# Clustered attention in front of two expert blocks: the cluster chain computed in PSUM, and a new order of the attention

## The chip, the cores and the metric

The kernel runs on one core of a Trainium2 chip. TensorE (PE) multiplies matrices into PSUM; VectorE (DVE), ScalarE (ACT) and GpSimd (POOL) work element by element; SyncE's queue (SP) issues the transfers. The metric is the device time of one execution in microseconds (us), as the median of several.

## The reference

Three parts follow one another. The first is attention for 2 batches x 8 heads, 768 tokens of 64 numbers, in which a query sees only the keys of its own cluster:

```python
q_assign = argmax(q_n . c_n)      # 16 centroids per head
k_assign = argmax(k_n . c_n)
mask = q_assign[:, None] == k_assign[None, :]
scores = where(mask, scale * q @ k.T, -1e9)
attn = softmax(scores);  out = attn @ v
```

The second is a mixture of experts: each of the 1,536 tokens (512 numbers) goes to the best of 8 experts (512 to 1024, relu, back to 512), and is weighted by two gates. The third is a dense layer pair (512 to 2048 and back) with a piecewise quadratic activation. All products use pairs of fp16 numbers (a high and a low half), so that their sums come close to fp32.

## The kernel before

**The attention** has 16 heads (`NH`), of which each goes through these steps, with 768 tokens as 6 tiles (`NT`) of 128:

- `load_kq`, `load_v`: SP loads k, q and v. `kq_hi` (ACT) rounds k and q to fp16, `kq_lo` takes the rest (fp32 minus fp16, 768 numbers per partition). `v_hi` and `v_lo` do the same for v (384 numbers). `a_dma` transposes the halves, `dup` copies the high halves into the tile `kq`.
- `logits`: PE multiplies with the centroids into `LG`, 192 columns of the PSUM tile `m_bank` (12 groups of 16 clusters: 6 of k, 6 of q). The same bank also holds the router's logits `LGX`, its ranks `RK` and one column `ZC`.
- `assign`, **the cluster chain** on DVE: the largest logit (L391), where it is reached (L394), times falling weights (L397), the largest of these, which is the first index (L400). From this q gets a one-hot row (L404) times 32768 (L406), and k the difference to its largest (L405). The results go into 16 columns of `kq`, and `b_dma` transposes the tile to `bT`.
- `s1`, `s1_max`: PE computes the masked scores of a tile of queries and DVE takes their maximum (L421, `mq`). `aug`, three DVE instructions on six columns (L426, L429, L431), turns the maxima into two more columns of `kq`; `q2_dma` transposes them.
- `st`: PE computes the scores again, transposed and with the maximum subtracted; `p_exp` (ACT) takes the exponential; `p_hi` (ACT or DVE) and `p_lo` (POOL or DVE, L462) split it into fp16 halves; `pv` multiplies with V, and `evac` (DVE, L492 to L496) divides by the sum and stores to `x_all`.

After head 8 the first batch is routed (`xsplit`, `xt_dma`, `lgx`, `gating`, `scatter`), after head 16 the second. Then the buffers of the attention are closed, and the experts and the dense layers follow.

**The order** of the attention's instructions comes from a planner, the class `Steps`, which runs while the program is built. Each step has a rank, engines that could take it with a duration each (`alts`), the steps it waits for, and places in rings of buffers that it takes and frees (`RINGS`; `lg`, the place of the logits, is 1). The planner keeps a clock for each engine, takes among the steps that could start within `eps` of the earliest the one with the lowest rank, and moves a step to its second engine where this ends it earlier by more than `gain`. The ranks are head number times 6 plus a constant of the kind of step (`R`) and a correction of single heads (`OFF`). Each engine executes its instructions in the order in which the planner issued them, and waits with semaphores for the others.

Of the kernel before, what the change touches and what calls it, by code (L numbers as in the profile page):

```python
# [30 lines left out]


class Steps:

    def __init__(self, rings):
        self.ready, self.order = [], []
        self.cap, self.freed = rings, {r: [] for r in rings}

    def add(self, rank, alts, fn, deps=(), take=(), free=(), lat=0.12, cols=None):


        o = dict(cols=cols, rank=rank, alts=alts, fn=fn, wait=0, at=0.0, take=take, free=free, lat=lat, next=[], end=None, slot={})
        for d in deps:
            if d is not None:
                d["next"].append(o)
                o["wait"] += 1
        if not o["wait"]:
            self.ready.append(o)  # L50
        return o

    def run(self, eps, gain):
        self.gain = gain
        busy, count, tick = {}, {}, 10.24 / 3
        while self.ready:
            pick = {}
            for o in self.ready:
                at = o["at"]
                for r in o["take"]:  # L60
                    f, n = self.freed[r], len(self.freed[r]) - self.cap[r]
                    if n >= 0:
# [15 lines left out]
            d = o["alts"][e]  # L78
# [41 lines left out]
def build(tc, q, k, v, centroids, w_gate, w_og, w1, w2, w_in, w_out, out):  # L120
    nc = tc.nc
# [248 lines left out]

    def dup(i):
        nc.vector.tensor_copy(out=kq[i % NKQ][:, :, :, 0:D].rearrange("p z t d -> p t z d"), in_=a_t[i][:, :, 0::3, :])

# [14 lines left out]
    def assign(i):  # L388

        mx = sm.tile([128, 2 * NT, 1], F32, tag="mx", name="mx")  # L390
        nc.vector.tensor_reduce(out=mx, in_=LG, axis=AX.X, op=ALU.max)  # L391
        yield
        eq = sm.tile([128, 2 * NT, NCL], F16, tag="eq", name="eq")
        nc.vector.tensor_tensor(out=eq, in0=LG, in1=mx.to_broadcast([128, 2 * NT, NCL]), op=ALU.is_equal)  # L394
        yield
        w = sm.tile([128, 2 * NT, NCL], F16, tag="w", name="w")
        nc.vector.tensor_tensor(out=w, in0=eq, in1=wt.to_broadcast([128, 2 * NT, NCL]), op=ALU.mult)  # L397
        yield
        m2 = sm.tile([128, 2 * NT, 1], F16, tag="m2", name="m2")
        nc.vector.tensor_reduce(out=m2, in_=w, axis=AX.X, op=ALU.max)  # L400
        yield
        oh = sm.tile([128, NT, NCL], F16, tag="oh", name="oh")
        x = kq[i % NKQ]
        nc.vector.tensor_tensor(out=oh, in0=w[:, NT:], in1=m2[:, NT:].to_broadcast([128, NT, NCL]), op=ALU.is_equal)  # L404
        nc.vector.tensor_tensor(out=x[:, 0, :, D:KS1], in0=w[:, 0:NT], in1=m2[:, 0:NT].to_broadcast([128, NT, NCL]), op=ALU.subtract)  # L405
        nc.vector.tensor_scalar(out=x[:, 1, :, D:KS1], in0=oh, scalar1=32768.0, scalar2=None, op0=ALU.mult)  # L406
        yield
# [15 lines left out]
    def aug(i, ts):  # L423

        m1 = sm.tile([128, NT, 1], F32, tag="m1", name="m1")[:, ts]
        nc.vector.tensor_scalar(out=m1[:, :, 0], in0=mq[:, i, ts], scalar1=-(2.0 ** 22), scalar2=-LN8 / SCALE, op0=ALU.max, op1=ALU.add)  # L426
# [364 lines left out]
    T = Steps(RINGS)  # L791
    R = dict(ld=-58.49, spl=-21.9, as_=-13.26, s1=-12.92, st=0, pv=3.78, hi=39.69, lo=30.55, v=31.52, la=4, rt0=23.34, rt1=-59.11, rt2=-5.38, l0=3)

    def chain(rank, gen, times, deps, fused, free):

        if fused:
            return T.add(rank, {"DVE": sum(times) + 0.13 * len(times)}, lambda e: [0 for _ in gen], deps, free=sum(free.values(), []))
        for n, t in enumerate(times):
            deps = [T.add(rank, {"DVE": t}, lambda e: next(gen), deps, free=free.get(n, ()))]
        return deps[0]  # L800

    FUSE = 0
    FLIP = set()
# [28 lines left out]
    for n, t in enumerate((1.3, 0.4, 0.25, 1.0, 0.35, 0.35, 0.4, 0.45, 0.1)):  # L832
# [5 lines left out]
    oc = T.add(-70, {"DVE": 1.4}, lambda e: [next(gc) for _ in range(7)], [oc])  # L838
    OFF = dict(st3=-3.12, s12=2.44, st2=-18.54, spl2=21.47, spl14=-28.12, s13=-2.76, s114=-4.75, as_15=-8.49, st1=-0.38,
               as_3=-3.72, st13=-1.49, s10=-18.85, as_14=-5.57, as_13=-26.13, st15=2.07, st14=2.24, as_2=-16.55, as_1=-11.58,  # L840
               s11=-11.74, spl3=1.1, spl0=-7.87, spl1=8.29, spl13=3.16, spl15=-8.66, as_0=2.02)
    for i in range(NH):
# [7 lines left out]
        hi = T.add(g + sp, {"ACT": 0.73}, do(kq_hi, i), [l], ["a"])  # L850
        lo = T.add(g + sp, {"POOL": 1.6, "DVE": 0.9} if i else {"DVE": 0.9}, on(kq_lo, i), [hi], free=[(l, "kqf")])
        if i == 0:
# [9 lines left out]
        if i == 0:  # L862
            wx = T.add(-25, {"ACT": 1.4}, do(warm, AF.Exp), [ad, cd])
        du = T.add(g + sp + 2, {"DVE": 0.27}, do(dup, i), [hi, pd, old(NKQ, "q2"), None if i else oc])
# [18 lines left out]
        for n in range(0, NT, NT2 if i in SPLIT else NT):  # L883
            ts = slice(n, n + NT2 if i in SPLIT else NT)
            a3 = chain(g + s1r + ts.stop - 1, aug(i, ts), (0.07, 0.07, 0.07), [ms[ts.stop - 1]], i < FUSE, {})
            if i in FLIP:
# [11 lines left out]
        for c in range(NT):  # L898
# [40 lines left out]
    for h in range(2):  # L939
# [379 lines left out]
```

## Time and profile before

| | |
|---|---|
| median of 3 runs | 726.38 us (724.6 to 728.76) |
| the profiled execution | 722.04 us, span 720.3 us |
| PE, DVE, ACT, POOL busy over the span | 609.2, 488.8, 380.5, 345.3 us |
| mean granted clock of TensorE | 0.934 |
| attention, from the start to its last evacuation | about 269 us |
| DMA, whole span | 96.29 MB |

An engine counts as busy from an instruction's start to its end, and what holds an instruction up after its start is counted in it. The granted clock is a share of the full 2.4 GHz; at half it is 1.2 GHz. Names such as L462 are lines of the kernel before.

### The profile page before, as it was taken

The numbers are of one execution on the slowest core, as the hardware profiler recorded it, in microseconds if no ns is written. First come the engines' busy times: TensorE is split into PE (matmuls) and PEld (weight loads), VectorE is DVE, ScalarE is ACT, GpSimd is POOL, SyncE is SP. The second block draws the span as 40 slices with busy tenths as digits, with TensorE's granted clock in tenths as the row PEclk, the third lists the DMA queues.
The fourth block names the chain that finished last, engine by engine and source line by source line (L and its number), as shares of the span: only waits on it lengthen the run. The fifth ranks groups of instructions, "written<-read, shape, count | busy, mean of one in ns | idle before, by whom it ended". The sixth has DMA issues, their size and how long they took to land. (4 is left out here: it accounts for less than half of the span.)

```text
span 720.3 us, 14223 instructions
## 1 busy us (share of the span) xinstructions
PE 609.2 (85%) x5574; PEld 388.1 (54%) x5574; DVE 488.8 (68%) x877; ACT 380.5 (53%) x599; POOL 345.3 (48%) x291
## 2 busy tenths in 40 slices
PE   1688698778888780889898789899899999999996
PEld 1256465545565460668888779544344444444442
DVE  7899989998998985477798578399981555510000
ACT  4167757666766740587586688166642544410000
POOL 7176857575766543135566343067751544421001
PEclk9989979888998885899999999999999999999999
DMA  8958487686733066999999997044650000000000
GB/s 206 194 122 194 99 176 160 155 160 123 136 68 124 15 101 165 288 313 279 202 273 177 238 311 236 7 151 142 180 171 29 30 1 0 1 15 29 15 29 30
DMA packets 142170, 96.29 MB, mean 134 GB/s; under 512 B 97168, under 2 KB 127888, under 8 KB 142096
## 3 DMA queue, kind: packets, MB, share of 16 engines
q1 hardware_dynamic: 139744, 88.60, 51.0%
q0 software_dynamic: 2352, 6.70, 2.5%
q8 instruction: 47, 0.77, 0.5%
q14 instruction: 27, 0.22, 0.1%
HBM read 59.84 MB, written 12.29 MB: 100 GB/s over the span
## 5 line engine op out<-in xcount | busy, mean ns | idle before, releaser
L462 POOL TENSOR_TENSOR pl<-p,ph 128x768 f16<-128x768 f32 x69 | 116.1, 1694 | 72.9 <-ACT ph L456 43.6
L451 ACT ACTIVATE p<-st 128x768 f32<-128x768 f32 x96 | 76.6, 809 | 75.3 <-PE st L447 67.2
L421 DVE TENSOR_REDUCE mq<-s 128x1 f32<-128x768 f32 x96 | 89.5, 945 | 11.7 <-PE s L416 11.1
L446 PE MATMUL st<-aT 128*128 128x384 f16 x192 | 69.7, 363 | 27.7 <-DVE mq L421 27.6
L1232 POOL TENSOR_TENSOR gt<-gx,gt 128x512 f16<-128x512 f32 x48 | 55.4, 1160 | 72.9 <-ACT gt L1231 72.9
L1217 PE MATMUL mps<-x,wih 128*128 128x512 f16 x192 | 73.5, 383 | 3.2 <-PEq L1172 3.2
L484 PE MATMUL pv<-vh,pl 128*128 128x65 f16 x576 | 70.2, 204 | 4.8 <-DVE pl L462 4.8
L1242 PE MATMUL ops<-woh,gt 128*128 128x512 f16 x192 | 72.8, 379 | 1.5 <-DVE gx L1230 1.5
L1224 DVE TENSOR_SCALAR cl<-mps 128x512 f32<-128x512 f32 x48 | 33.1, 689 | 60.2 <-PE mps L1219 60.2
L1218 PE MATMUL mps<-x,wih 128*128 128x512 f16 x192 | 73.4, 382 | 0.0
L1243 PE MATMUL ops<-wol,gt 128*128 128x512 f16 x192 | 72.8, 379 | 0.7 <-POOL wol L1023 0.5
L1219 PE MATMUL mps<-x,wil 128*128 128x512 f16 x192 | 73.3, 382 | 0.0
L1226 ACT ACTIVATE sq<-cl,c 128x512 f32<-128x512 f32 x48 | 34.6, 721 | 73.0 <-DVE cl L1224 73.0
L1244 PE MATMUL ops<-woh,gt 128*128 128x512 f16 x192 | 72.8, 379 | 0.0
L482 PE MATMUL pv<-vh,ph 128*128 128x65 f16 x576 | 70.9, 205 | 0.0
L483 PE MATMUL pv<-vl,ph 128*128 128x64 f16 x576 | 70.5, 203 | 0.0
L447 PE MATMUL st<-q2T,bT 82*128 82x384 f16 x192 | 69.8, 363 | 0.0
L1086 PE MATMUL yps<-hT,w2h 128*128 128x176 f16 (+6 forms) x256 | 64.3, 258 | 6.4 <-ACT hT L1076 3.9
L1087 PE MATMUL yps<-hT,w2h 128*128 128x176 f16 (+6 forms) x256 | 64.1, 257 | 5.8 <-DVE hT L1077 5.4
L456 ACT ACTIVATE ph<-p 128x768 f16<-128x768 f32 x83 | 68.2, 840 | 0.6
L1070 PE MATMUL hps<-xt,w1h 128*128 128x176 f16 (+6 forms) x256 | 52.9, 260 | 17.5 <-ACT w1h L993 15.2
L1088 PE MATMUL yps<-hT,w2l 128*128 128x176 f16 (+6 forms) x256 | 64.0, 257 | 1.1 <-DVE w2l L994 1.1
(222 smaller groups left out, 1532.4 us busy)
## 6 DMA issues: line engine op xcount, KB each, us to landing
stg<-in_moe_w_dram SPq DMA_DIRECT2D x64, 512.0 KB, 6.8
stg<-in_moe_w_in_dram SPq DMA_DIRECT2D x16, 512.0 KB, 5.8
stg<-in_moe_w_out_dram SPq DMA_DIRECT2D x16, 512.0 KB, 3.7
xs<-zrow SPq DMA_DIRECT2D x16, 288.0 KB, 2.8
kqf<-in_k_dram SPq DMA_DIRECT2D x16, 192.0 KB, 3.3
kqf<-in_q_dram SPq DMA_DIRECT2D x16, 192.0 KB, 3.2
vf<-in_v_dram SPq DMA_DIRECT2D x16, 192.0 KB, 3.2
xs<-zrow SPq DMA_DIRECT2D x8, 108.0 KB, 3.8
```

Of the source, the lines that this page charges most:

```text
L421: nc.vector.tensor_reduce(out=mq[:, i, t:t + 1], in_=lg_t.pop((i, t))[:, :, 0:HS], axis=AX.XY, op=ALU.max)
L451: nc.scalar.activation(out=p.rearrange("p (e s) -> p e s", e=2), in_=lg_t.pop(("t", i, c))[:, :, 0:HS], func=AF.Exp, scale=SCALE)
L462: eng.tensor_tensor(out=pl_t[i, c], in0=p_t.pop((i, c)), in1=ph_t[i, c], op=ALU.subtract)
L482: nc.tensor.matmul(out=x[:, 0:D + 1], lhsT=ph[:, sl], rhs=a[:, c, 0:D + 1], start=False, stop=False)
L483: nc.tensor.matmul(out=x[:, 0:D], lhsT=ph[:, sl], rhs=b[:, c, :], start=False, stop=False)
L484: nc.tensor.matmul(out=x[:, 0:D + 1], lhsT=pl[:, sl], rhs=a[:, c, 0:D + 1], start=False, stop=end and (j, t) == (1, NT2 - 1))
L1217: nc.tensor.matmul(out=p, lhsT=wih[:, kk, f], rhs=x2[:, 0, kk, c], start=(kk == 0), stop=False)
L1218: nc.tensor.matmul(out=p, lhsT=wih[:, kk, f], rhs=x2[:, 1, kk, c], start=False, stop=False)
L1219: nc.tensor.matmul(out=p, lhsT=wil[:, kk, f], rhs=x2[:, 0, kk, c], start=False, stop=(kk == KD - 1))
L1242: nc.tensor.matmul(out=p, lhsT=gt[:, 0, f, c], rhs=woh[:, f, :], start=(f == 0), stop=False)
L1243: nc.tensor.matmul(out=p, lhsT=gt[:, 0, f, c], rhs=wol[:, f, :], start=False, stop=False)
L1244: nc.tensor.matmul(out=p, lhsT=gt[:, 1, f, c], rhs=woh[:, f, :], start=False, stop=(f == KF2 - 1))
```

## The change

`assign` now works in place on `LG` in PSUM, in fp32, with seven instructions that are seven steps of the planner (before, the last three were one step). `aug` keeps its intermediate `m1` in six columns of `m_bank` instead of SBUF. The place of the logits is freed after the last of the seven steps, not after the second. `dup` takes its engine as an argument (DVE). `kq_lo` has one engine: POOL, and DVE for head 0. `v_lo` has one engine: DVE. `p_lo` has one engine: DVE for tiles 2 and 5, POOL for the four others. In the planner a step can name the engines for which it holds a common port (`port`): a step on DVE that does so starts only after the last such step of POOL, and the other way round. A step can name a bank: PE and DVE then take turns on it. Several durations, the constants `R` and `OFF`, `eps` and `gain` are new.

```diff
+R = dict(ld=-43.75, spl=-20.42, as_=-12.8, s1=-14.8, st=-2.85, pv=1.25, hi=60.29, lo=27.4, v=35.43, la=4, rt0=20.57,
+           rt1=5.77, rt2=57.35, l0=3)
+OFF = dict(st3=-3.39, s12=2.27, spl2=36.38, spl14=-26.15, as_3=-3.12, s10=-15.85, as_13=-26.23, st15=28.86, st14=11.11,
...
+EPS, GAIN = 0.066, 0.58
+LOV, VLV, KQV = (2, 5), True, False
...
                     for e, d in o["alts"].items():
                         t = max(at, busy.get(e, 0.0))
+                        if e in o["port"]:
+                            t = max(t, port[other[e]])
+                        if o["bank"]:
+                            t = max([t] + [b for x, b in banks.get(o["bank"], {}).items() if x != e])
...
+            if e in o["port"]:
+                port[e] = end
+            if o["bank"]:
+                banks.setdefault(o["bank"], {})[e] = end + 0.1
...
+    o3 = o2 + (NT + 1) * E + 1
+    M1 = m_bank[:, o3:o3 + NT].rearrange("p (t o) -> p t o", o=1)
...
     def assign(i):
+        bc = lambda a, n=2 * NT: a.to_broadcast([128, n, NCL])
         mx = sm.tile([128, 2 * NT, 1], F32, tag="mx", name="mx")
         nc.vector.tensor_reduce(out=mx, in_=LG, axis=AX.X, op=ALU.max)
         yield
-        eq = sm.tile([128, 2 * NT, NCL], F16, tag="eq", name="eq")
-        nc.vector.tensor_tensor(out=eq, in0=LG, in1=mx.to_broadcast([128, 2 * NT, NCL]), op=ALU.is_equal)
-        yield
-        w = sm.tile([128, 2 * NT, NCL], F16, tag="w", name="w")
-        nc.vector.tensor_tensor(out=w, in0=eq, in1=wt.to_broadcast([128, 2 * NT, NCL]), op=ALU.mult)
-        yield
-        m2 = sm.tile([128, 2 * NT, 1], F16, tag="m2", name="m2")
-        nc.vector.tensor_reduce(out=m2, in_=w, axis=AX.X, op=ALU.max)
-        yield
-        oh = sm.tile([128, NT, NCL], F16, tag="oh", name="oh")
+        nc.vector.tensor_tensor(out=LG, in0=LG, in1=bc(mx), op=ALU.is_equal)
+        yield
+        nc.vector.tensor_tensor(out=LG, in0=LG, in1=bc(wt), op=ALU.mult)
+        yield
+        m2 = sm.tile([128, 2 * NT, 1], F32, tag="m2", name="m2")
+        nc.vector.tensor_reduce(out=m2, in_=LG, axis=AX.X, op=ALU.max)
+        yield
         x = kq[i % NKQ]
-        nc.vector.tensor_tensor(out=oh, in0=w[:, NT:], in1=m2[:, NT:].to_broadcast([128, NT, NCL]), op=ALU.is_equal)
-        nc.vector.tensor_tensor(out=x[:, 0, :, D:KS1], in0=w[:, 0:NT], in1=m2[:, 0:NT].to_broadcast([128, NT, NCL]), op=ALU.subtract)
-        nc.vector.tensor_scalar(out=x[:, 1, :, D:KS1], in0=oh, scalar1=32768.0, scalar2=None, op0=ALU.mult)
+        lk, lq = LG[:, 0:NT], LG[:, NT:]
+        nc.vector.tensor_tensor(out=lq, in0=lq, in1=bc(m2[:, NT:], NT), op=ALU.subtract)
+        yield
+        nc.vector.tensor_tensor(out=x[:, 0, :, D:KS1], in0=lk, in1=bc(m2[:, 0:NT], NT), op=ALU.subtract)
+        yield
+        nc.vector.tensor_scalar(out=x[:, 1, :, D:KS1], in0=lq, scalar1=0.0, scalar2=32768.0, op0=ALU.is_equal, op1=ALU.mult)
         yield
...
     def aug(i, ts):
-        m1 = sm.tile([128, NT, 1], F32, tag="m1", name="m1")[:, ts]
+        m1 = M1[:, ts]
...
-        lo = T.add(g + sp, {"POOL": 1.6, "DVE": 0.9} if i else {"DVE": 0.9}, on(kq_lo, i), [hi], free=[(l, "kqf")])
+        lo = T.add(g + sp, {"DVE": 0.9} if KQV or not i else {"POOL": 1.66}, on(kq_lo, i), [hi], free=[(l, "kqf")], port=BOTH)
...
-        vl_ = T.add(g + R["v"], {"POOL": 0.87, "DVE": 0.47}, on(v_lo, i), [vh_], free=[(lv, "vf")])
-        lg = T.add(g + as_, {"PE": 0.6}, do(logits, i), [ad, cd], ["lg"], cols=-384)
-        x5 = chain(g + as_, assign(i), (0.27, 0.27, 0.17, 0.27, 0.45), [lg, rw, du, pd], i < FUSE, {1: [(lg, "lg")]})
+        vl_ = T.add(g + R["v"], {"DVE": 0.5} if VLV else {"POOL": 0.95}, on(v_lo, i), [vh_], free=[(lv, "vf")], port=BOTH)
+        lg = T.add(g + as_, {"PE": 0.6}, do(logits, i), [ad, cd], ["lg"], cols=-384, bank="m")
+        x5 = chain(g + as_, assign(i), (0.29, 0.29, 0.29, 0.29, 0.2, 0.2, 0.2), [lg, rw, du, pd], {6: [(lg, "lg")]}, "m")
...
-            ph = T.add(g + st_ + c + R["hi"], {"ACT": 0.73, "DVE": 0.55}, on(p_hi, i, c), [e], ["ph"])
-            pl = T.add(g + st_ + c + R["lo"], {"POOL": 1.6, "DVE": 0.87}, on(p_lo, i, c), [ph], ["pl"], free=[(e, "p")])
+            ph = T.add(g + st_ + c + R["hi"], {"ACT": 0.73, "DVE": 0.5}, on(p_hi, i, c), [e], ["ph"], port=("DVE",))
+            pl = T.add(g + st_ + c + R["lo"], {"DVE": 0.95} if c in LOV else {"POOL": 1.66}, on(p_lo, i, c), [ph], ["pl"], free=[(e, "p")], port=BOTH)
...
-    T.run(0.062, 0.97)
+    T.run(EPS, GAIN)
```

## Rows read from the trace of the kernel before

**Rows 1.** Busy time by stretch: start:end, length, each engine, granted clock, DMA share, GB/s.

```profile
0.00:15.00 15.00, 1.56 (x34) 1.30 (x35) 10.29 (x27) 7.62 (x14) 11.40 (x43) 1.00 0.78 203
15.00:250.00 235.00, 186.76 (x2516) 125.44 (x2514) 217.53 (x378) 148.42 (x203) 149.27 (x108) 0.89 0.64 135
250.00:269.00 19.00, 17.14 (x313) 12.92 (x311) 15.46 (x21) 10.13 (x14) 9.18 (x6) 0.84 0.57 95
269.00:282.00 13.00, 1.76 (x28) 1.12 (x24) 10.04 (x65) 1.68 (x6) 7.16 (x8) 0.66 0.31 114
282.00:720.00 438.00, 401.99 (x2696) 247.31 (x2696) 235.47 (x388) 212.70 (x362) 168.32 (x128) 0.97 0.49 133
```

**Rows 2.** Groups by line, DVE, 0 to 270 us: busy us, mean ns, idle before.

```profile
L462 DVE TENSOR_TENSOR pl<-p,ph 128x768 f16<-128x768 f32 x27 | 35.2, 1311 | 0.4
L429 DVE TENSOR_SCALAR kq<-m 128x6 f16<-128x6 f32 (+1 forms) x18 | 13.3, 739 | 0.0
L426 DVE TENSOR_SCALAR m<-mq 128x6 f32<-128x6 f32 (+1 forms) x18 | 10.4, 579 | 0.1
L397 DVE TENSOR_TENSOR w<-eq,wt 128x192 f16<-128x192 f16 x16 | 10.1, 634 | 0.2
L404 DVE TENSOR_TENSOR oh<-w,m 128x96 f16<-128x96 f16 x16 | 9.1, 567 | 0.1
L431 DVE SCALAR_TENSOR_TENSOR kq<-m,kq 128x6 f16<-128x6 f32 (+1 forms) x18 | 8.4, 474 | 0.1
L405 DVE TENSOR_TENSOR kq<-w,m 128x96 f16<-128x96 f16 x16 | 7.5, 471 | 0.0
L406 DVE TENSOR_SCALAR kq<-oh 128x96 f16<-128x96 f16 x16 | 5.7, 357 | 0.0
L378 DVE TENSOR_TENSOR vl<-vf,vh 128x384 f16<-128x384 f32 x9 | 4.8, 546 | 0.0
```

**Rows 3.** Single lines on DVE: ns min/median/max, first and last start in us.

```profile
L397 DVE TENSOR_TENSOR w<-eq,wt x16: 245/259/1732, 14.9 to 208.2; 128x192 f16<-128x192 f16 x16
L426 DVE TENSOR_SCALAR m<-mq x18: 152/172/1637, 24.5 to 242.1; 128x6 f32<-128x6 f32 x14, 128x3 f32<-128x3 f32 x4
L429 DVE TENSOR_SCALAR kq<-m x18: 156/183/1622, 25.5 to 243.5; 128x6 f16<-128x6 f32 x14, 128x3 f16<-128x3 f32 x4
L462 DVE TENSOR_TENSOR pl<-p,ph x27: 942/954/2433, 42.9 to 263.8; 128x768 f16<-128x768 f32 x27
L372 DVE COPY kq<-a x16: 344/554/2932, 8.2 to 177.2; 128x768 f16<-128x768 f16 x16
L394 DVE TENSOR_TENSOR eq<-m_bank,mx x16: 342/348/359, 14.4 to 207.8; 128x192 f16<-128x192 f32 x16
L492 DVE TENSOR_SCALAR r<-pv x17: 147/153/166, 58.8 to 269.0; 128x6 f32<-128x6 f32 x15, 128x3 f32<-128x3 f32 x2
```

**Rows 4.** Timeline of POOL, then of DVE: start us, duration us.

```profile
136.20 3.33 POOL L462 TENSOR_TENSOR pl<-p,ph 128x768 f16<-128x768 f32 x2 [4.19 <-ACT ph L456]
...
137.95 1.62 DVE L429 TENSOR_SCALAR kq<-m 128x6 f16<-128x6 f32 x1
```

**Rows 5.** Groups by line, POOL, 0 to 270 us.

```profile
L462 POOL TENSOR_TENSOR pl<-p,ph 128x768 f16<-128x768 f32 x69 | 116.1, 1694 | 72.9 <-ACT ph L456 43.6 <-DVE ph L458 7.4 <-PE st L447 6.6
L351 POOL TENSOR_TENSOR a<-kqf,a 128x768 f16<-128x768 f32 x13 | 21.7, 1675 | 13.6 <-DMA vf<-in_v_dram 7.3 <-ACT a L347 6.3
L378 POOL TENSOR_TENSOR vl<-vf,vh 128x384 f16<-128x384 f32 x7 | 7.0, 1007 | 0.8 <-ACT vh L375 0.8
```

**Rows 6.** Waits of PE, 0 to 270 us: us in total, times, longest.

```profile
PE st L446 <- DVE mq L421: 27.6, 19, 4.7
...
PE m_bank L385 <- DVE eq L394: 3.2, 1, 3.2
```

**Rows 7.** Timeline of DVE, one head's chain: its second and last instruction.

```profile
123.84 0.36 DVE L394 TENSOR_TENSOR eq<-m_bank,mx 128x192 f16<-128x192 f32 x1
...
133.42 0.17 DVE L406 TENSOR_SCALAR kq<-oh 128x96 f16<-128x96 f16 x1
```

More of the change, by code (lines that the diff above doesn't have):

```diff
@@ L30, with add @@
 NWIN = 20
+R = dict(ld=-43.75, spl=-20.42, as_=-12.8, s1=-14.8, st=-2.85, pv=1.25, hi=60.29, lo=27.4, v=35.43, la=4, rt0=20.57,
+           rt1=5.77, rt2=57.35, l0=3)
+OFF = dict(st3=-3.39, s12=2.27, spl2=36.38, spl14=-26.15, as_3=-3.12, s10=-15.85, as_13=-26.23, st15=28.86, st14=11.11,
+           as_2=-15.51, s11=-11.75, s115=18.09, st2=0.31, s113=2.4, s13=-4.32, spl0=13.81, as_14=-6.15, spl1=3.22,
+           s114=0.6, spl3=0.26, as_0=-0.18, spl13=3.11, spl15=-5.48)
+EPS, GAIN = 0.066, 0.58
+LOV, VLV, KQV = (2, 5), True, False
 class Steps:
     def __init__(self, rings):
-        self.ready, self.order = [], []
+        self.ready = []
         self.cap, self.freed = rings, {r: [] for r in rings}
-    def add(self, rank, alts, fn, deps=(), take=(), free=(), lat=0.12, cols=None):
-        o = dict(cols=cols, rank=rank, alts=alts, fn=fn, wait=0, at=0.0, take=take, free=free, lat=lat, next=[], end=None, slot={})
+    def add(self, rank, alts, fn, deps=(), take=(), free=(), lat=0.12, cols=None, port=(), bank=None):
+        o = dict(cols=cols, port=port, bank=bank, rank=rank, alts=alts, fn=fn, wait=0, at=0.0, take=take, free=free, lat=lat, next=[], end=None, slot={})
         for d in deps:
@@ L55, in run @@
         busy, count, tick = {}, {}, 10.24 / 3
+        port, banks = {"DVE": 0.0, "POOL": 0.0}, {}
+        other = dict(DVE="POOL", POOL="DVE")
         while self.ready:
@@ L86, in run @@
             o["end"] = end
+            o["on"] = (e, t)
+            if e in o["port"]:
+                port[e] = end
+            if o["bank"]:
+                banks.setdefault(o["bank"], {})[e] = end + 0.1
             for r in o["take"]:
@@ L369, in a_dma, with dup @@
         nc.sync.dma_start_transpose(out=at_of(i).rearrange("p t z c -> p (t z) c"), in_=a_t[i].rearrange("p t z d -> p (t z d)"))
-    def dup(i):
-        nc.vector.tensor_copy(out=kq[i % NKQ][:, :, :, 0:D].rearrange("p z t d -> p t z d"), in_=a_t[i][:, :, 0::3, :])
+    def dup(i, eng):
+        eng.tensor_copy(out=kq[i % NKQ][:, :, :, 0:D].rearrange("p z t d -> p t z d"), in_=a_t[i][:, :, 0::3, :])
     def v_hi(i):
@@ L791, in build, with chain @@
     T = Steps(RINGS)
[L792 to L797, printed above, removed]
+    def chain(rank, gen, times, deps, free, bank=None):
         for n, t in enumerate(times):
-            deps = [T.add(rank, {"DVE": t}, lambda e: next(gen), deps, free=free.get(n, ()))]
+            deps = [T.add(rank, {"DVE": t}, lambda e: next(gen), deps, free=free.get(n, ()), bank=bank, lat=0.2)]
         return deps[0]
-    FUSE = 0
+    BOTH = ("DVE", "POOL")
     FLIP = set()
@@ L838, in build @@
     oc = T.add(-70, {"DVE": 1.4}, lambda e: [next(gc) for _ in range(7)], [oc])
-    OFF = dict(st3=-3.12, s12=2.44, st2=-18.54, spl2=21.47, spl14=-28.12, s13=-2.76, s114=-4.75, as_15=-8.49, st1=-0.38,
-               as_3=-3.72, st13=-1.49, s10=-18.85, as_14=-5.57, as_13=-26.13, st15=2.07, st14=2.24, as_2=-16.55, as_1=-11.58,
-               s11=-11.74, spl3=1.1, spl0=-7.87, spl1=8.29, spl13=3.16, spl15=-8.66, as_0=2.02)
     for i in range(NH):
@@ L863, in build @@
             wx = T.add(-25, {"ACT": 1.4}, do(warm, AF.Exp), [ad, cd])
-        du = T.add(g + sp + 2, {"DVE": 0.27}, do(dup, i), [hi, pd, old(NKQ, "q2"), None if i else oc])
+        du = T.add(g + sp + 2, {"DVE": 0.32}, on(dup, i), [hi, pd, old(NKQ, "q2"), None if i else oc], port=BOTH)
         z = T.add(g + sp + 2, {"SP": 0.0}, None, [ad, du], free=[(hi, "a")], lat=0.0)
         vh_ = T.add(g + R["v"], {"ACT": 0.41}, do(v_hi, i), [lv, pd, old(NV, "evac")])
-        vl_ = T.add(g + R["v"], {"POOL": 0.87, "DVE": 0.47}, on(v_lo, i), [vh_], free=[(lv, "vf")])
-        lg = T.add(g + as_, {"PE": 0.6}, do(logits, i), [ad, cd], ["lg"], cols=-384)
-        x5 = chain(g + as_, assign(i), (0.27, 0.27, 0.17, 0.27, 0.45), [lg, rw, du, pd], i < FUSE, {1: [(lg, "lg")]})
+        vl_ = T.add(g + R["v"], {"DVE": 0.5} if VLV else {"POOL": 0.95}, on(v_lo, i), [vh_], free=[(lv, "vf")], port=BOTH)
+        lg = T.add(g + as_, {"PE": 0.6}, do(logits, i), [ad, cd], ["lg"], cols=-384, bank="m")
+        x5 = chain(g + as_, assign(i), (0.29, 0.29, 0.29, 0.29, 0.2, 0.2, 0.2), [lg, rw, du, pd], {6: [(lg, "lg")]}, "m")
         if i in FLIP:
@@ L884, in build @@
             ts = slice(n, n + NT2 if i in SPLIT else NT)
-            a3 = chain(g + s1r + ts.stop - 1, aug(i, ts), (0.07, 0.07, 0.07), [ms[ts.stop - 1]], i < FUSE, {})
+            a3 = chain(g + s1r + ts.stop - 1, aug(i, ts), (0.1, 0.13, 0.13), [ms[ts.stop - 1]], {}, "m")
             if i in FLIP:
@@ L908, in build @@
             if last and c == NT2 - 1:
-                O["half"] = chain(g, evac(i, slice(0, NT2)), (0.07, 0.1, 0.25), prev, False, {})
-        O["evac", i] = chain(g + st_ + R["pv"] - 1, evac(i, slice(NT2, NT) if last else slice(0, NT)), (0.07, 0.1, 0.25 if last else 0.47), prev, False,
+                O["half"] = chain(g, evac(i, slice(0, NT2)), (0.13, 0.1, 0.3), prev, {})
+        O["evac", i] = chain(g + st_ + R["pv"] - 1, evac(i, slice(NT2, NT) if last else slice(0, NT)), (0.13, 0.1, 0.3 if last else 0.5), prev,
                              {2: [(pvs[NT2], "s")] if last else [(pvs[0], "pv")]})
@@ L931, in build @@
         sp = [T.add(g, {"ACT": 0.73}, do(xsplit_hi, b, j), [ev(b * H + 2 * j), ev(b * H + 2 * j + 1)] + last) for j in range(js)]
-        sp = [T.add(g, {"POOL": 1.6, "DVE": 0.87}, on(xsplit_lo, b, j), [sp[j]]) for j in range(js)]
+        sp = [T.add(g, {"POOL": 1.66, "DVE": 0.87}, on(xsplit_lo, b, j), [sp[j]], port=BOTH) for j in range(js)]
         xt = [T.add(g + XS * u, {"SP": 2.4}, do(xt_dma, u), sp + [pz] + last, lat=DL) for u in range(NT // 2)]
@@ L944, in build @@
         o3 = T.add(g, {"ACT": 0.37}, do(xl_hi, h), [o, last[-1]])
-        o3 = T.add(g, {"POOL": 0.85, "DVE": 0.45}, on(xl_lo, h), [o3])
+        o3 = T.add(g, {"POOL": 0.85, "DVE": 0.45}, on(xl_lo, h), [o3], port=BOTH)
         lx = [T.add(g, {"PE": 0.1}, do(lgx, t, [KD - 1]), [o2, cp]) for t in range(h * NT2, (h + 1) * NT2)]
```

## The prediction

> **What bounds the kernel now.** I read the view of stretches first [rows 1]. Everything the diff touches runs in the attention, from 0 to about 269 us; the 13 us after it (the last routing) and the rest up to 720 us only begin later or earlier with it. In the 235 us from 15 to 250, VectorE (DVE) is busy 217.5 us, 93%; TensorE (PE) 186.8 us, 79%, at a mean granted clock of 0.89; ScalarE (ACT) 148 us and GpSimd (POOL) 149 us, 64% at most. So DVE sets the pace. Over the three stretches up to 269 us DVE is busy 10.3 + 217.5 + 15.5 = 243.3 us and idle 25.7 us; POOL is busy 11.4 + 149.3 + 9.2 = 169.9 us; PE 1.6 + 186.8 + 17.1 = 205.5 us.
>
> Then the groups of DVE's instructions [rows 2] against the shortest, median and longest of the same lines [rows 3]. The reader is to see tiny instructions with huge means: L429 writes six numbers per partition, its median is 183 ns, its mean 739, its longest 1,622. The timeline of both engines shows why [rows 4]: a POOL pair of p_lo runs from 136.20 to 139.53, and DVE's L429, begun at 137.95, ends at 139.57, with the POOL instruction. It is held, and counted as busy, until POOL is through: a p_lo on POOL takes 1,694 ns in the mean [rows 5], and the longest of L397, L426 and L429 are 1,622 to 1,732 [rows 3]. Two lines that read PSUM are never held: L394 (PSUM and a small SBUF operand) stays within 342 and 359 ns, L492 within 147 and 166 [rows 3].
>
> **The cluster chain in PSUM.** Held time is count times (mean minus median). L397: 16 x (634 - 259) = 6.0 us. L404 and L405, similar fp16 instructions, with the same 259: 16 x (567 - 259) = 4.9 and 16 x (471 - 259) = 3.4. L406 with L429's 183: 16 x (357 - 183) = 2.8. L426: 18 x (579 - 172) = 7.3. L429: 18 x (739 - 183) = 10.0. L431: 18 x (474 - 183) = 5.2. Sum: 39.6 us of DVE [rows 2, 3]. After the change each of these has an operand in PSUM and at most one tensor in SBUF, the shape of L394 and L492, so I count all 39.6 as gone. One form has no row: L426 will read SBUF and write PSUM. It may stay held as now (7.3 us kept) or not at all; I take not at all, since the held lines all have their operands wholly in SBUF, and keep 7.3 for the range. The Trainium skill's page "SBUF — State Buffer", section "Who interferes with whom", says that a VectorE instruction with at most one SBUF input and outside the two-port modes does not contend with GpSimd, and that the loser of the shared port blocks for the other's whole instruction; L429's longest next to a POOL instruction agrees, and by that rule the 7.3 us would go as well.
>
> What the chain pays: the product moves from fp16 in SBUF (259 ns) to fp32 in PSUM, like L394 (348): 16 x 0.089 = +1.4 us. The three half-size instructions (96 elements) took 0.26 + 0.26 + 0.18 = 0.70 us; between L492's 153 ns at six columns and L394's 348 at 192, 96 columns lie near 250, so 0.75: 16 x 0.05 = +0.8 us (bounds 0, and +5.5 at 348 each). The two reductions and aug's three instructions of six columns cost what they cost (153 ns against 172 and 183): 0. The skill's page "VectorE: DVE Perf Modes", "Why PSUM operands drop a tier", speaks against moving fp16 work to PSUM, as the fast packed mode goes; the rows agree, with 348 against 259 ns, and it is the +1.4 us above.
>
> **Work between DVE and POOL.** p_lo goes from 27 on DVE and 69 on POOL to a fixed 32 and 64 (blocks 2 and 5 of each of 16 heads): DVE +5 x 0.954 = +4.8, POOL -5 x 1.694 = -8.5. v_lo goes wholly to DVE, from 9 and 7: DVE +7 x 0.546 = +3.8, POOL -7 x 1.007 = -7.0. kq_lo goes to POOL but for head 0: of three on DVE two leave, at p_lo's 0.954 (same shape) -1.9; POOL +2 x 1.675 = +3.4. [rows 2, 3, 5] The choice of p_hi between ACT and DVE stays the planner's.
>
> **Sum for DVE:** -39.6 + 1.4 + 0.8 + 4.8 + 3.8 - 1.9 = -30.7 us, from 243.3 to 212.6. POOL falls by 12.1 to 157.8.
>
> **The other side: what POOL and DVE share.** If POOL's instructions and DVE's all-SBUF ones exclude each other, they are one queue. Now: POOL 169.9, plus, unheld, p_lo 27 x 0.954 = 25.8, the assign lines 16 x (3 x 0.259 + 0.183) = 15.4, aug 18 x (0.172 + 0.183 + 0.183) = 9.7, dup 16 x 0.344 = 5.5, v_lo 9 x 0.546 = 4.9: 231.2 us of 269, 86%. After: 157.8 + 32 x 0.954 + 5.5 + 16 x 0.546 = 202.5, that is 28.7 us less; at the same 86% it needs 235.5 us, 33.5 less. Both counts agree on about 30 us.
>
> **The new order.** The planner now keeps DVE and POOL apart on that port and PE and DVE apart on the bank of the chain; its ranks are all new. It can't be costed from rows, only bounded. The middle stretch holds 217.5 - 30.7 = 186.8 us of DVE work, by chance just what PE has. At today's 93% it would take 200.8 us (a gain of 34), at 87% 214.7 us (a gain of 20). DVE reached 93% while PE stood at 79% and could be kept ahead; with both at the same load, each in its own order, I take 89%: 209.9 us, a gain of 25.1. Loads, transposes and the zeroing of rows keep their number and sizes and only shift rank on SP's queue; POOL's scatters keep their dependencies. The tail from 269 us on is the same chain, and the weights that follow load when the attention's buffers are closed, so the whole rest moves up as a block: 0 gained or lost there.
>
> Against the profiled execution (722.0 us, span 720.3) that is 696.9. The median of the runs shown is 726.4, 4.4 above it; the forecast for the median is 726.4 - 25.1 = 701.3, **701 us**.
>
> **The rivals.**
> *PE becomes the bound.* PE waits 27.6 us for DVE's mq and 3.2 for the chain [rows 6], which the change can give back, but its 186.8 us of work stays, part of it at the half clock (mean 0.89). In the last stretch before 269 us PE reached 90% at 0.84. If it only holds 85% in the middle, that is 219.7 us: a gain of 15, **711 us**. For it: PE needs nearly DVE's new load. Against: PE's clock falls where PE waits, and those waits shrink.
> *The held time moves.* The DVE instructions that still exclude POOL are 32 + 16 + 16 = 64, now 52. If each met a POOL instruction at random (64% busy, half of 1.65 us left) it would be held 0.53 us, 34 us in all, where p_lo alone is now held 27 x (1.311 - 0.954) = 9.6 and dup about 16 x (0.554 - 0.344) = 3.4 by its median. Some 20 us would come back: a gain of 10, **716 us**. Against: the planner now sees the port.
> *Better than the sum.* If the port-aware order removes the held time of p_lo and dup too (about 13 us, of which I would credit 10) the gain is 41: **686 us**.
> *Slower: the bank is held longer.* The logits' place in PSUM used to come free after the second instruction of the chain; now only after the seventh. In one head the second began at 123.84 and the last ended at 133.59 [rows 7], nearly 10 us. PE works in order, so logits that come too early stop everything behind them: scores, products with V, then ACT and POOL. Today one such wait shows, of 3.2 us [rows 6]. With 15 heads it decides from a mean of 25.1 / 15 = 1.7 us a head; at 2.0, and with all of it on the path, the time is 726.4 - 25.1 + 30 = **731 us**. The skill's page "PSUM — Partial Sum Buffer", section "PSUM bank collisions raise a hardware error", would have software keep engines apart by whole banks: then also the router's logits and ranks, in the same bank as aug's new cell, wait for the chain, which is what this rival needs. Against: a head lasts 269 / 16 = 16.8 us, longer than the chain, and the planner models the wait.
> *No change:* the order gives the gain back by chance, **726 us**.
>
> **How the numbers follow.** Forecast (692 to 710) 0.50; better (680 to 692) 0.14; PE (710 to 716) 0.17; moved held time (716 to 722.7) 0.08; within 0.5% of 726.4 (about what a measurement of this kernel can tell) 0.04; slower 0.07. Faster is 0.50 + 0.14 + 0.17 + 0.08 = 0.89. The range from 686 to 722 leaves out the lower half of the better case (0.07) and same and slower (0.11), and it takes in the unknown costs: 7.3 for the PSUM-writing form and 4.7 more for the half-size instructions still leave a gain of 13.
>
> **What would show it.** Right: in the page of the changed kernel the chain's and aug's lines have means within 20% of their medians; DVE's busy time up to the last evacuation near 213 us; POOL's p_lo 64 times; that evacuation ends near 244 us; the part after it is as long as now. Wrong: m1's line still reaches 1.6 us; waits of PE for the chain's last line of over 25 us; DVE's p_lo or dup with a mean above 1.5 us; a granted clock below 0.85 from 15 us on; or idle time of DVE in the middle over 25 us, which would say that the order, not the held time, sets the end.

## The result, and the profile after

The changed kernel takes 703.31 us (median of 4 runs, 700.64 to 703.76) against 726.2 us: a ratio of 0.967, interval 0.964 to 0.971. The forecast was 701, in a range of 686 to 722. Its profiled execution took 703.17 us, span 701.4, against 722.04 and 720.3 before. An execution more than 1.5% above the fastest of its kernel counts as slow and is left out of the times and ratios below.

The view of stretches of the changed kernel, cut where its attention ends (before: [rows 1]):

```profile
0.00:15.00 15.00, 1.76 (x35) 1.26 (x36) 9.34 (x30) 8.98 (x16) 13.73 (x48) 1.00 0.81 215
15.00:235.00 220.00, 184.53 (x2527) 122.79 (x2523) 187.14 (x374) 155.07 (x214) 135.76 (x93) 0.88 0.67 143
235.00:255.00 20.00, 15.32 (x302) 13.23 (x301) 13.56 (x22) 10.47 (x16) 11.62 (x7) 0.76 0.57 95
255.00:268.00 13.00, 2.18 (x22) 1.62 (x22) 9.55 (x62) 1.64 (x6) 6.81 (x7) 0.50 0.32 117
```

DVE's busy time in the attention is 9.3 + 187.1 + 13.6 = 210.0 us; the forecast said 212.6. But the 187.1 us of the middle took 220 us: DVE is busy 85% there, not 93% as before and not the 89% that I had chosen, and its 32.9 us of idle time are above the 25 that the prediction had named as a sign that the order sets the end. In the timeline of DVE the last evacuation shows where the attention ends, here before (L496) and after (L520):

```profile
269.38 0.36 DVE L496 TENSOR_TENSOR x_all<-pv,r 128x192 f32<-128x192 f32 x1
...
254.75 0.36 DVE L520 TENSOR_TENSOR x_all<-pv,r 128x192 f32<-128x192 f32 x1
```

So the attention gained 269.7 - 255.1 = 14.6 us, not 25. The other 4.3 us of the span's 18.9 lie behind it, where nothing was changed, and the medians, with 22.9, show 4 more than the two profiled executions. That the total came out near the forecast is in part luck: these 8 us were not in it.

The groups of DVE in the attention after the change (before: [rows 2]), then single lines with shortest, median and longest (before: [rows 3]):

```profile
L486 DVE TENSOR_TENSOR pl<-p,ph 128x768 f16<-128x768 f32 x32 | 40.2, 1266 | 0.6 <-ACT ph L480 0.6
L401 DVE TENSOR_TENSOR vl<-vf,vh 128x384 f16<-128x384 f32 x16 | 12.5, 788 | 0.4 <-ACT vh L398 0.4
L395 DVE COPY kq<-a 128x768 f16<-128x768 f16 x16 | 10.6, 675 | 0.3 <-ACT a L370 0.3
L419 DVE TENSOR_TENSOR m_bank<-m_bank,wt 128x192 f32<-128x192 f32 x16 | 5.8, 360 | 0.6 <-PE m_bank L580 0.3
L426 DVE TENSOR_TENSOR m_bank<-m_bank,m 128x96 f32<-128x96 f32 x16 | 4.2, 261 | 0.8 <-PE m_bank L580 0.5
L428 DVE TENSOR_TENSOR kq<-m_bank,m 128x96 f16<-128x96 f32 x16 | 4.0, 250 | 0.2
L430 DVE TENSOR_SCALAR kq<-m_bank 128x96 f16<-128x96 f32 x16 | 4.0, 248 | 0.1
L455 DVE SCALAR_TENSOR_TENSOR kq<-m_bank,kq 128x6 f16<-128x6 f32 (+1 forms) x18 | 3.2, 175 | 0.3
L453 DVE TENSOR_SCALAR kq<-m_bank 128x6 f16<-128x6 f32 (+1 forms) x18 | 3.1, 174 | 0.3
L450 DVE TENSOR_SCALAR m_bank<-mq 128x6 f32<-128x6 f32 (+1 forms) x18 | 2.9, 163 | 0.4
```

```profile
L450 DVE TENSOR_SCALAR m_bank<-mq x18: 151/166/169, 23.1 to 234.2; 128x6 f32<-128x6 f32 x14, 128x3 f32<-128x3 f32 x4
L486 DVE TENSOR_TENSOR pl<-p,ph x32: 941/949/2394, 37.0 to 250.5; 128x768 f16<-128x768 f32 x32
```

The aug line that writes six numbers (L453, before L429) fell from a mean of 739 ns to 174. L450, the form for which no row existed (SBUF in, PSUM out), never exceeds 169 ns, though 11 of its 18 began while an instruction ran on POOL: the 7.3 us that I had kept for the range are gone too. What is still held works in SBUF alone: p_lo, mean 1,266 ns against a median of 949, v_lo (788 against 548) and dup (L395, 675 against 366), about 19 us in all.

POOL's groups (before: [rows 5]), ACT's p_hi, and the waits of DVE (L421 is the line of the kernel before) and of PE (before: [rows 6]):

```profile
L486 POOL TENSOR_TENSOR pl<-p,ph 128x768 f16<-128x768 f32 x64 | 112.8, 1780 | 54.4 <-ACT ph L480 41.2 <-issue 4.1 <-PE s L440 3.2
L374 POOL TENSOR_TENSOR a<-kqf,a 128x768 f16<-128x768 f32 x15 | 24.9, 1657 | 23.6 <-ACT a L370 23.6
...
L480 ACT ACTIVATE ph<-p 128x768 f16<-128x768 f32 x96 | 77.5, 847 | 0.8
...
DVE mq L421 <- PE s L416: 11.1, 13, 2.5
...
DVE mq L445 <- PE s L440: 23.0, 29, 3.7
...
PE st L470 <- DVE mq L445: 3.2, 6, 1.4
PE m_bank L408 <- DVE kq L430: 1.6, 1, 1.6
```

The wait turned round: before, PE waited 27.6 us for DVE's maxima; now 3.2, and DVE waits 23.0 us for PE's scores (11.1 before). All 96 p_hi are on ACT, where 13 had been on DVE. PE waits for the chain's end (L430) once, for 1.6 us.

### The profile page after: what moved, and what is told of

It is laid out like the page before. It is cut to its first block, busy times and chain, and to the rows that moved or that the text cites. A ratio compares the mean times of both kernels' runs of the same rounds, so it can differ in the third digit from the quotient of the medians.

```text
span 701.4 us, 14212 instructions
## 1 busy us (share of the span) xinstructions
PE 605.7 (86%) x5574; PEld 387.1 (55%) x5574; DVE 452.4 (64%) x874; ACT 388.9 (55%) x612; POOL 335.5 (48%) x281
## 5 line engine op out<-in xcount | busy, mean ns | idle before, releaser
L486 POOL TENSOR_TENSOR pl<-p,ph 128x768 f16<-128x768 f32 x64 | 112.8, 1780 | 54.4 <-ACT ph L480 41.2
L480 ACT ACTIVATE ph<-p 128x768 f16<-128x768 f32 x96 | 77.5, 847 | 0.8
L508 PE MATMUL pv<-vh,pl 128*128 128x65 f16 x576 | 68.7, 203 | 10.1 <-DVE pl L486 10.1
L1088 PE MATMUL hps<-xt,w1h 128*128 128x176 f16 (+6 forms) x256 | 54.4, 265 | 15.4 <-DMA xt<-xs 14.2
```

The costliest lines, as they stand in the source:

```text
L480: nc.scalar.activation(out=ph_t[i, c], in_=p_t[i, c], func=AF.Copy)
L486: eng.tensor_tensor(out=pl_t[i, c], in0=p_t.pop((i, c)), in1=ph_t[i, c], op=ALU.subtract)
```

## The experiments

Each is named by its label. "The attention ends" is the end of the last evacuation in the timeline of its profiled execution, in us; the last column adds up the steps of the granted clock up to there. All times are medians, and the ratios are to the kernel before on the same chip; there it took 724 to 726 us, and single runs of it 718 to 737. The end of the attention repeats better: two executions each of the changed kernel and of e4's differ in it by 0.5 and 1.3 us. A time of a single run (a7, e5, e8) can be off by 10 us.

| kernel | runs | time, us | ratio to before (interval) | attention ends | of it at half clock |
|---|---|---|---|---|---|
| before | 4 | 726.2 | 1 | 269.7 | 58 |
| changed | 4 | 703.31 | 0.967 (0.964 to 0.971) | 255.1 | 61 |
| a1: changed, again | 4 of 6 | 706.50 | 0.968 (0.960 to 0.977) | 254.6 | 51 |
| e1: new order, chain and m1 in SBUF | 9 of 10 | 720.07 | 0.992 (0.987 to 0.997) | 265.1 | 48 |
| e2: new order, m1 in SBUF | 4 | 715.59 | 0.989 (0.982 to 0.997) | 263.3 | 51 |
| e4: chain in PSUM, old order | 3 of 4 | 693.65 | 0.963 (0.950 to 0.976) | 240.0 | 31 |
| a2: the same, again | 4 of 6 | 697.86 | 0.962 (0.956 to 0.967) | 238.7 | 27 |
| a4: old rules, new ranks | 4 | 703.5 | 0.967 (0.960 to 0.975) | 247.8 | 38 |
| a3: new rules, old ranks | 9 of 10 | 721.59 | 0.997 (0.993 to 1.001) | 267.6 | 70 |
| a6: a2 and the port rule | 3 of 4 | 710.3 | 0.979 (0.968 to 0.990) | 265.2 | 47 |
| a7: a2 and the fixed engines | 1 | 722.62 | | 264.6 | 51 |
| e3: changed, no port rule | 4 | 738.09 | 1.019 (1.001 to 1.038) | 282.0 | 75 |
| e5: changed, less TensorE work | 1 | 699.36 | | 249.9 | 61 |
| e8: changed, fillers on TensorE | 1 | 754.58 | | 298.3 | 68 |

The profile of a6 is of an execution at the top of its four (716.64 us, against 703.91 at the bottom), so its end is on the late side.

**e1_chain_in_sbuf: the operands go back, the order stays.**

```diff
-        nc.vector.tensor_tensor(out=LG, in0=LG, in1=bc(mx), op=ALU.is_equal)
+        eq = sm.tile([128, 2 * NT, NCL], F16, tag="eq", name="eq")
+        nc.vector.tensor_tensor(out=eq, in0=LG, in1=mx.to_broadcast([128, 2 * NT, NCL]), op=ALU.is_equal)
...
-        m1 = M1[:, ts]
+        m1 = sm.tile([128, NT, 1], F32, tag="m1", name="m1")[:, ts]
```

> The changed kernel with exactly its new order, but with the cluster chain and aug's intermediate back in SBUF (fp16, as before). Theory A (the gain is the held time of the small all-SBUF instructions): the seven lines are held again by GpSimd's instructions, some 35 to 40 us of VectorE in all, VectorE's busy time up to the last evacuation rises from 210 to about 245 us, and the attention, which ends at 255 us in the changed kernel and at 270 in the kernel before, ends at 268 to 285 us; the time is 718 to 735 us. Rival B (the gain is the new order, the place of the operands counts little): the attention ends within 3 us of 255 and the time is 700 to 707 us.

Measured: 720.07 us, the attention ends at 265.1 us. The groups of DVE of this kernel, two lines of aug and one of the chain:

```profile
L454 DVE TENSOR_SCALAR kq<-m 128x6 f16<-128x6 f32 (+1 forms) x18 | 11.6, 643 | 0.1
...
L451 DVE TENSOR_SCALAR m<-mq 128x6 f32<-128x6 f32 (+1 forms) x18 | 8.4, 465 | 0.1
...
L420 DVE TENSOR_TENSOR w<-eq,wt 128x192 f16<-128x192 f16 x16 | 10.1, 629 | 0.2
```

The means are back. Over the seven lines count times (mean minus median) gives 35.5 us, as theory A said, and rival B falls. But these 35.5 us move the end by 10.0 us only, less than A's 13, and DVE's busy time up to there rises from 210 to 229 us, not to 245: p_lo, v_lo and dup are held less here and take 9.1 us less together. With its new order and the old operands the kernel gains 269.7 - 265.1 = 4.6 us over before.

**e2_m1_in_sbuf: only aug goes back.**

```diff
-        m1 = M1[:, ts]
+        m1 = sm.tile([128, NT, 1], F32, tag="m1", name="m1")[:, ts]
```

> The changed kernel with only aug's intermediate m1 back in SBUF; the cluster chain stays in PSUM and the order is the same. Theory A: the three small instructions of aug are held again, in sum 15 to 23 us of VectorE (they were held 22.5 us in the kernel before), and the attention ends 8 to 20 us later than 255 us, time 711 to 724 us. Rival B: these instructions are off the path, the attention ends within 3 us of 255 us, time 700 to 707 us.

Measured: 715.59 us, end at 263.3 us, 8.2 later. In this kernel's groups the three lines stand at 541, 646 and 350 ns (163, 174 and 175 in the changed kernel): 18 x (0.378 + 0.472 + 0.175) = 18.5 us.

```profile
L453 DVE TENSOR_SCALAR kq<-m 128x6 f16<-128x6 f32 (+1 forms) x18 | 11.6, 646 | 0.1
L450 DVE TENSOR_SCALAR m<-mq 128x6 f32<-128x6 f32 (+1 forms) x18 | 9.7, 541 | 0.1
...
L455 DVE SCALAR_TENSOR_TENSOR kq<-m,kq 128x6 f16<-128x6 f32 (+1 forms) x18 | 6.3, 350 | 0.2
```

So of the 10.0 us of e1, aug makes 8.2, and the chain's instructions, put back as well, the other 1.8, little more than a repeat can differ by. Aug stands between a head's last maximum and its second scores, where other work waits for it.

**e4_psum_chain_old_order and a2_psum_chain_old_order_again: the operands move, the order stays.** The kernel before, with the seven instructions on `LG` (the last three in one step, as they were) and `M1`; in the planner only the place of the logits is freed later. Up to the last evacuation the instructions of PE, DVE, ACT and POOL keep the order of the kernel before, but for one dup of DVE that comes three places earlier.

```diff
-        x5 = chain(g + as_, assign(i), (0.27, 0.27, 0.17, 0.27, 0.45), [lg, rw, du, pd], i < FUSE, {1: [(lg, "lg")]})
+        x5 = chain(g + as_, assign(i), (0.27, 0.27, 0.17, 0.27, 0.45), [lg, rw, du, pd], i < FUSE, {4: [(lg, "lg")]})
```

> The kernel before with its old planner constants and durations; only the cluster chain and aug's intermediate move to PSUM (the place of the logits comes free after the chain's last step). Theory A: VectorE loses the 40 us of held time, of which the old order, planned for other durations, turns 10 to 25 us into time: the attention ends at 245 to 260 us instead of 270, time 702 to 717 us. Rival B: the place of the operands counts little, the attention ends at 267 to 272 us, time 722 to 729 us. Rival C (the logits' place is held longer and TensorE waits for it): TensorE's waits for the chain's last line come to 15 us or more, and the time is 726 us or above.

> The chain in PSUM in the old order, again, on the chip of the changed kernel. Theory C: the attention ends at 238 to 246 us with 25 to 40 us at the half clock, the time is 690 to 699 us. Rival D: it ends near 255 us and the time is within 4 us of the changed kernel's.

> The changed kernel itself once more, for a comparison on one chip with the run next to it (the chain in PSUM in the old order), which on another chip took 695.6 us, with its attention ending at 240 us. Theory C (the chain in PSUM is the whole gain, and the new order gives half of it back because TensorE runs longer at the half clock): the attention ends at 252 to 258 us, with 50 us or more of it at the half clock, and the time is 5 to 15 us above its neighbour's. Rival D (the difference was the chip's): both times are within 4 us of each other.

Measured: the attention ends at 240.0 and at 238.7 us, earlier than theory A allowed and 15 us before the changed kernel's (255.1 and 254.6). On one chip, side by side, the medians are 697.86 (a2) and 706.50 us (a1), 8.6 apart, and the slowest of a2's counted runs (699.92) lies below the fastest of a1's (701.77); their intervals against before overlap a little, the ends of the attention do not come near each other. Theory C's part on the size holds, its cause is not shown by these runs; rivals B, C (in e4) and D fall. The stretches of a2, the second cut out of the first, and its last evacuation:

```profile
15.00:220.00 205.00, 176.00 (x2533) 118.39 (x2533) 189.88 (x380) 148.33 (x204) 153.12 (x106) 0.95 0.72 155
...
77.00:141.00 64.00, 57.01 (x933) 40.35 (x932) 62.95 (x125) 53.65 (x76) 57.97 (x34) 1.00 0.91 208
...
238.38 0.36 DVE L497 TENSOR_TENSOR x_all<-pv,r 128x192 f32<-128x192 f32 x1
```

DVE has 189.9 us of work in the middle, about the forecast's 186.8, at 93% as in the kernel before, and for 64 us at full clock 98%. PE's granted clock is 0.95 where the changed kernel has 0.88. Among the waits there is the one for the chain's last line (L407), which the slower rival was built on, but it is small:

```profile
PE st L447 <- DVE mq L422: 9.9, 14, 2.6
PE m_bank L387 <- DVE kq L407: 7.1, 2, 4.5
```

**a3_new_rules_old_ranks and a4_old_rules_new_ranks: what of the new order costs the 15 us.** a3 is the changed kernel with the constants `R`, `OFF`, `EPS` and `GAIN` of before; a4 is e4 with those of the changed kernel.

```diff
-EPS, GAIN = 0.066, 0.58
+EPS, GAIN = 0.062, 0.97
```

> The changed kernel with all its new rules (chain in PSUM, fixed engines, port and bank in the planner, new durations) but the ranks, head corrections and two thresholds of the kernel before. If the ranks are to blame for what the new order costs, the attention ends at 238 to 248 us; if the new rules are, at 252 us or later; ranks that were chosen for other rules may also end far later, as without the port rule (282 us).

> The chain in PSUM with the old rules of the planner (two engines to choose from, no port, no bank, old durations) but the new ranks, head corrections and thresholds. If the ranks are to blame, the attention ends at 252 us or later, as in the changed kernel; if the rules are, at 238 to 248 us.

Measured: 267.6 us for a3, 247.8 for a4. With the chain in PSUM in all four, the rules cost 28 us with the old ranks (239.4 to 267.6) and 7 with the new (247.8 to 254.9); the new ranks cost 8 with the old rules and win back 13 with the new. So by the marks set before (a4 meets its own by 0.2 us) the rules are to blame, most of all under the old ranks. The new ranks fit the new rules better than the old ranks do, but not so far that the pair reaches the old pair.

**a6_port_rule_alone and a7_fixed_engines_alone: which rule.**

```diff
+                        if e in o["port"]:
+                            t = max(t, port[other[e]])
...
-            pl = T.add(g + st_ + c + R["lo"], {"POOL": 1.6, "DVE": 0.87}, on(p_lo, i, c), [ph], ["pl"], free=[(e, "p")])
+            pl = T.add(g + st_ + c + R["lo"], {"DVE": 0.87} if c in (2, 5) else {"POOL": 1.6}, on(p_lo, i, c), [ph], ["pl"], free=[(e, "p")])
```

> The chain in PSUM in the old order (attention 239 to 240 us, 696 to 699 us) with one new rule, the port in the planner; each step still has its two engines, old ranks and durations. If the port rule is what the new order costs, the attention ends at 250 us or later; if the fixed engines are, it ends at 233 to 245 us; as the planner's estimates come nearer to the chip it could also gain up to 6 us.

> The chain in PSUM in the old order with one new rule, the fixed engines (tiles 2 and 5 of p_lo and all of v_lo on VectorE, kq_lo on GpSimd); no port rule, old ranks and durations. If the fixed engines are what the new order costs, the attention ends at 250 us or later, with TensorE at the half clock for 45 us or more; if the port rule is, at 235 to 246 us.

Measured: 265.2 and 264.6 us in the profiled executions. For the fixed engines that is 25 us more than in a2, by one run. For the port rule the profile shows too much, since it is of a6's slowest execution; by the medians, 710.3 against a2's 697.86 on another chip, the rule costs about 12 us. Each rule alone, put on the old ranks, costs time, so neither is the one culprit. For the port rule, POOL's groups show how:

```profile
L469 POOL TENSOR_TENSOR pl<-p,ph 128x768 f16<-128x768 f32 x92 | 149.4, 1649 | 20.8 <-ACT ph L463 19.3 <-issue 1.5
```

A planner that knows of the port, and may choose, hardly uses DVE for p_lo: 92 of 96 go to POOL, held time all but vanishes (1,649 ns in the mean), and POOL is busy 213 us of the attention, more than PE (205) and DVE (172). That it is now the bound is likely, but not shown. The changed kernel pays its 19 us of held time and has the shorter attention.

**e3_planner_without_port: the changed kernel without that rule.**

```diff
+        port = ()
         o = dict(cols=cols, port=port, bank=bank, rank=rank, ...
```

> The changed kernel, but the planner no longer keeps VectorE and GpSimd apart on their common port; the bank rule, ranks and durations stay. Theory A (what is left of the held time is p_lo, v_lo and dup on VectorE; the planner's port rule keeps part of it away): their held time rises from about 20 to over 30 us and the attention ends 3 to 12 us later than 255 us, time 706 to 716 us. Rival B (the port rule is idle): the same held time, within 2 us of 255, time 701 to 706 us.

Measured: 738.09 us, end at 282.0 us, far beyond both expectations; p_lo on DVE rises to 1,468 ns in the mean, and 26 p_hi, at 1,122 ns, go to DVE.

```profile
L487 DVE TENSOR_TENSOR pl<-p,ph 128x768 f16<-128x768 f32 x32 | 47.0, 1468 | 1.1 <-ACT ph L481 0.7
L483 DVE CAST ph<-p 128x768 f16<-128x768 f32 x26 | 28.9, 1122 | 9.3 <-ACT p L476 9.3
```

The new ranks with fixed engines need the port rule. That the rule is worth 27 us in general does not follow: on the old ranks it costs about 12 (a6).

**e5_less_tensor_work and e8_fillers: is TensorE the pace in the new order, and is its clock the cause?**

```diff
-                nc.tensor.matmul(out=x[:, 0:D], lhsT=ph[:, sl], rhs=b[:, c, :], start=False, stop=False)
```

> The changed kernel without the products of p's high half with v's low half (576 of TensorE's 2,562 matmuls of the attention; that part of the sum is left out), same order. Theory C (in the new order TensorE, slowed by the half clock, sets the pace): the attention ends at 240 to 248 us instead of 255. Rival E (VectorE still sets the pace): it ends within 3 us of 255 us, and TensorE waits more instead.

```diff
+        if not end:
+            for _ in range(2):
+                nc.tensor.matmul(out=fl(o), lhsT=zrow[0:1, 0:128], rhs=zrow[0:1, 0:o.shape[1] * (D + 1)], start=False, stop=False)
```

> The changed kernel with work added to TensorE: after each tile's products with V, unless it is a head's last, two matmuls of zeros over 390 columns that add nothing (150 to 160 more matmuls, some 26 us at full clock), same order. Theory C1 (the half clock comes from TensorE's gaps and is a cause of the lost time): the fillers close gaps, the half clock of the attention falls from 51 to 61 us to below 35, and the attention ends at or before 255 us despite the added work. Rival C2 (the half clock is only a sign of waits, TensorE has no spare time): the attention ends at 262 to 280 us.

Measured: with less work the attention ends 5.2 us earlier, for 12.9 us less of PE's busy time (188.7 against 201.6), between both expectations. With the fillers (L512) it ends at 298.3 us, later than C2 said, 43.2 us for their 45.1 us of busy time (26 had been expected), and the half clock does not fall (68 us): from 87.3 to 118.0 us the granted clock stays at half with PE busy 98%.

```profile
L512 PE MATMUL pv<-zrow 1*128 1x390 f16 (+1 forms) x158 | 45.1, 370 | 0.0
```

C1 falls in this form: these fillers, one row of zeros deep, do not raise the clock. C2 holds in part: in the new order PE has little time to spare, and what is added to it comes out almost whole at the end, while what is taken away gives 40% back. In e5 DVE is then busy 88% of the middle, and still waits 16.8 us for PE's scores, so that neither engine alone sets the pace. Two stretches of the changed kernel itself, one at half and one at full clock, fit that:

```profile
91.80:112.30 20.50, 17.83 (x168) 10.64 (x166) 16.51 (x33) 12.84 (x18) 12.52 (x8) 0.50 0.94 218
139.60:170.30 30.70, 27.80 (x468) 20.03 (x466) 26.62 (x46) 26.42 (x35) 23.63 (x14) 1.00 0.61 109
```

At half clock PE does 8.2 matmuls per us and is busy 87%, with DVE at 81 and ACT at 63%; at full clock 15.2, with DVE at 87 and ACT at 86%. In the table, among the runs with the whole chain in PSUM and all of the work, the half clock and the attention's end rise together in seven of nine, from 27 us with 238.7 to 75 us with 282.0; a6, where POOL is the busiest engine, and a7 end 10 us and more later than their half clock would put them.

## Why the prediction came out right, and where it was off

- **What bounds the kernel.** Shown for the kernel before: DVE, held by POOL. Without the held time of these lines, in the same order, the attention is 30 us shorter (e4, a2).
- **The chain in PSUM.** Counted: -39.6 + 1.4 + 0.8 = -37.4 us of DVE. Measured over the ten lines: 81.1 us before, 44.2 after, -36.9. The small terms were near: the product 360 ns (348 foreseen), the half-size three 261, 250 and 248 (250 foreseen). L450 in its new form is not held: 169 ns at most. The Trainium skill's page "SBUF — State Buffer", section "Who interferes with whom", says so of an instruction with at most one SBUF input outside the two-port modes, and the trace agrees. What aug costs with `m1` back in SBUF, e2 shows: 8.2 us at the end.
- **Work between DVE and POOL.** The counts came as read from the diff (32 and 64, 16, 15). Left to the planner's choice, and out of both sums, was p_hi: its 13 on DVE, 11.2 us busy, all went to ACT. That DVE's sum still came out at 210.0 against 212.6 has two held groups on the other side: v_lo, whose mean went from 546 to 788 ns (16 x 0.242 = 3.9 us), and small instructions of the first batch's routing, up to 1.3 us each.
- **The new order: the mis-sized term.** I took 89% for DVE in the middle and so 5.6 us less than the sum's 30.7. Measured is 85%, and 187.1 us in 220: the attention ends at 255.1 us where 244 was forecast and gained 14.6 us, while the old order kept its 93% and gained 30. The new order costs 15 us of the attention (the changed kernel against e4, and a1 against a2), almost three times the term. This is the rival "PE becomes the bound", worked out with 85% and a gain of 15: DVE waits 23.0 us for PE's scores, which fits it, though e5 and e8 suggest that PE and DVE bound it together. The argument against it, that PE's clock falls where PE waits and those waits shrink, did not hold here: the waits for DVE's maxima fell from 27.6 to 3.2 us, and the half clock went from 58 to 61 us (51 in a1).
- **The tail, counted at 0.** From the last evacuation to the end it takes 450.6 us before, 446.3 in the changed kernel's profile and 454.6 in a1's; over all fourteen traces 446.3 to 457.6. Its gain of 4.3 us is inside that spread and can't be credited to the change. With the 4 us of the medians it made up, by luck, for most of what the order had lost: on the chip of a1 the changed kernel's median is only 18.6 us below that of the kernel before (706.50 against 725.12).
- **The other rivals.** Held time did move, but by less than the 20 us priced: 3.9 us in v_lo, and on POOL's side p_lo's mean rose from 1,694 to 1,780 ns; the slower one, logits waiting for the chain, showed 1.6 us (7.1 in a2) where 25 were needed, and the router's products on the same bank held the chain up by 1.6 us in all (L419, L422, L426).

What stays open: why the new order leaves PE at half clock for 51 to 61 us where the old one, with the chain in PSUM, has 27 to 31. That half clock and length go together is shown for seven of nine runs; which comes first is not. In a2's stretches at half clock PE is busy 92% (25.1 of 27.2 us), in the changed kernel's 80% (48.6 of 60.9), so there it waits for others even while it is slow. The fillers did not settle it, and no kernel was tried in which the clock alone differs.

## What to carry to other kernels

Look for small instructions with a mean far above their median, see in the timeline whose instruction ends with theirs, and give them an operand in PSUM; the change of DVE's time, counted line by line, was right to 2%. Then change the operands with the order held fixed before the order is planned anew: here the first alone is worth 30 us of the attention, both together 15, and the version to keep is e4, the old order with the chain in PSUM (693.7 and 697.9 us, against 703.3 and 706.5). A planner's constants fit its rules as a whole: two new rules, each alone on the old constants, cost about 12 and 25 us.

## What the runs showed of the hardware

A DVE instruction that reads SBUF and writes PSUM was not held by POOL in 18 of 18 cases (169 ns at most; 11 of them began while an instruction ran on POOL), where the same one into SBUF reached 1.6 us. Not everything in SBUF alone is held: in the kernel before, the reduction L400 took 333 to 354 ns and the reciprocal L494 173 to 191, though 4 of 16 and 6 of 17 began while an instruction ran on POOL. Matmuls of zeros, one row deep and 390 columns wide, filled PE to 91% of the middle stretch and left the half clock at 68 us of the attention; for 30.7 us it stayed with PE busy 98%. And the unchanged 446 to 458 us behind the attention differ by 11 us between executions of the same instructions, more than half of what the changed part gained.
